# Cosformer attention and a mixture of adapters on one core: q scaled by a diagonal on TensorE, k scaled on GpSimd, attention numerators in row tiles

## The chip, the cores and the metric

The kernel runs on one core of one Trainium2 chip. The metric is the device time of one execution in microseconds (us). A core has a matrix engine (TensorE, PE in the profile; its weight loads are shown apart as PEld), VectorE (DVE), ScalarE (ACT), GpSimd (POOL), a queue engine (SyncE, SP) and 16 DMA engines. Each engine executes its own instructions in the order in which they were put in its queue, and semaphores make an engine wait for another. Matmul results land in PSUM (eight banks of 2 KB per partition), everything else is in SBUF.

## The reference

Inputs are q, k and v of shape 8 x 8 x 576 x 64 (batch, head, position, channel), and the weights of eight adapters of rank 16 on 512 channels. Linear attention with cosine weights comes first:

```python
theta = np.pi / 2.0 * pos / S
def phi(x, c, s):
    r = np.maximum(x, 0.0)
    return np.concatenate([r * c, r * s], axis=-1)
q_p = phi(q, cos_w, sin_w)
k_p = phi(k, cos_w, sin_w)
kv = np.einsum('bhsf,bhsd->bhfd', k_p, v)
z = np.sum(k_p, axis=2)
num = np.einsum('bhsf,bhfd->bhsd', q_p, kv)
den = np.einsum('bhsf,bhf->bhs', q_p, z)[..., None] + 1e-06
return (num / den).astype(np.float32)
```

Its output, as 4608 rows x of 512 channels, goes through the adapters: the two largest of eight gate logits `x @ w_gate` are chosen, a softmax over the two gives weights w, and the result is `x + sum over the two of w * ((x @ A[e]) @ B[e])`.

## The kernel before

**Layout.** A load puts one batch of q, k or v in SBUF as [128, G=4, NS=9, 64]: the partitions are two heads of a pair times 64 position blocks r, and position r * 9 + s lies at index s. So one s of one batch is a set of 64 positions of all eight heads. cos_tab and sin_tab hold, for each partition and s, the cosine and the sine of the position.

**A tile n** (NT = 36) is 128 output rows: two sets of 64. Nine tiles make a pair of batches 2m and 2m+1: four tiles of the first batch, four of the second, and a mixed one (s = 8 of both).

**k side, once per batch.** scale_k writes kp = max(k * cos, 0) and max(k * sin, 0), one instruction each per s (L141; batch 0 has the cosines on ScalarE, L139). kv (L155) multiplies kp with v and a column of ones, eight matmuls per s, each over the 64 partitions of one head, so that the two heads of a pair stand in different row halves of the array; it sums in kvz (two PSUM banks) over all nine s. kv_out copies the sums to SBUF (L162).

**q side, per tile.** scale_q (L168) makes four scaled pieces qp on VectorE; transp_q (L177) transposes them in eight matmuls with the identity into qpTp, a single bf16 PSUM bank; evac_q (L184) copies that to SBUF in one instruction of 1024 elements. numden (L197, L202) puts a small constant in the denominators and multiplies: per head one matmul over all 128 features (64 of cosine, 64 of sine). Its result nd takes two PSUM banks and has one buffer.

**Behind it.** normalise (L209, L211) divides, giving xt. transp_x (L219) and evac_x (L225) make its transpose, logits (L239) multiplies that with adapters and gate weights together. For a group of three tiles gate_a (L248 to L257), gate_sig (Sigmoid, L265) and gate_b (L272, L274) choose and weight the adapters, transp_z (L282) and evac_z (L288) transpose the result. delta (L294, L295) adds x and the adapters' second product in PSUM (dx, one bank), evac_o (L303) copies it out, store (L311) writes it by two DMAs on SP.

**Order.** The order within each engine's queue is written out by hand: the loop over n calls the helpers one after another, and each engine takes its instructions in that order. Iteration n holds normalise(n), the numerators of n+1, the transposes of x(n), scaling and transposing of q(n+2), and an older tile's delta. In the kernel before, logits of a whole group come in one iteration, gate_a at its end, gate_sig at the top of the next and gate_b at that one's end. Lists (scale_at, kv_at) place three s of scale_k and kv in six of nine iterations. All loads but k of batch 0 and the weights are issued by GpSimd, which converts fp32 to bf16 on the way, all ahead of the loop; the weights come by SP as fp32 and are cast on VectorE (L327 to L330).

## Time and profile before

| | us |
|---|---|
| median of 3 runs (148.26 to 149.88) | 149.34 |
| the profiled execution | 149.11 |
| its span, first to last instruction | 147.3 |

The profile is of one execution. Its page gives the busy time of each engine, then the chain of work that ended last, followed back from the last instruction, then the costliest groups of instructions: line, engine, operation, output and inputs, shapes, count, then busy us and mean ns of one, and the idle time of the engine ahead of them with what ended it. A timeline row gives the start in us, the duration of the row, the engine, the line and the operation; "x8" are eight instructions in a row, and what stands in brackets is the engine's idle time before, with its releaser. Durations overlap on an engine: where one instruction's end is not waited for, the next starts earlier, and the step from start to start is what the engine needs. TensorE's granted clock is 0.98 over the span, and the DMA engines are over 90% busy for the first 85 us or so:

| us from the start | PE | DVE | ACT | POOL |
|---|---|---|---|---|
| 50 to 60, busy | 8.09 | 9.36 | 6.22 | 1.48 |
| 100 to 110, busy | 8.14 | 8.72 | 6.72 | 0.00 |

### The profile page before, as it was taken

How to read it: one execution, taken by the hardware profiler on the slowest of the kernel's cores; microseconds unless marked ns; L12 is line 12 of the kernel's file. 1: busy time of each engine (PE TensorE's matmuls, PEld its weight loads, DVE VectorE, ACT ScalarE, POOL GpSimd, SP SyncE). 2: the span in 40 equal slices, each digit the busy share in tenths (PEclk: the TensorE clock that was granted, in tenths of full speed). 3: DMA queues.
4: the chain of work that ended last, by engine and by line, in shares of the span. 5: the costliest groups of instructions: out<-in, count | busy, mean ns of one | idle time of the engine just before them, and what ended most of it. 6: DMA issues, size and time to landing. Idle time of an engine off the chain costs nothing.

```text
span 147.3 us, 4206 instructions
## 1 busy us (share of the span) xinstructions
PE 103.9 (71%) x1652; PEld 73.6 (50%) x1652; DVE 110.7 (75%) x483; ACT 88.5 (60%) x143; POOL 18.1 (12%) x31
## 2 busy tenths in 40 slices
PE   0019589856878788778788788688877887777540
PEld 0018468744655555555466456346654556464110
DVE  3251799868798798798896987987988987866400
ACT  7370155767457757596476566875584577875540
POOL 6922322232222222000000000000000000000000
PEclk9999999999999999999999999999999999999975
DMA  4999999999999999999999933143333332534783
GB/s 100 320 204 233 208 209 207 208 208 207 207 239 237 236 238 240 237 237 242 261 229 231 232 77 83 46 104 71 75 72 76 71 87 65 122 93 111 166 205 92
DMA packets 19780, 25.00 MB, mean 170 GB/s; under 512 B 2736, under 2 KB 14512, under 8 KB 19760
## 3 DMA queue, kind: packets, MB, share of 16 engines
q0 software_dynamic: 12144, 13.57, 53.7%
q1 hardware_dynamic: 7616, 11.16, 29.1%
q8 instruction: 13, 0.21, 0.6%
q14 instruction: 7, 0.06, 0.1%
HBM read 28.85 MB, written 9.44 MB: 260 GB/s over the span
## 4 chain that ended last, share of the span: by engine, by line
DVE 43%; PE 29%; ACT 13%; DMA 6%; issue 5%; ACTq 0%; POOLq 0%
DVE kp L141 15%; DVE xt L211 11%; PE xz L219 7%; DMA v<-in_v_dram 6%; PE za L239 5%; PE qpTp L177 5%; ACT qpT L184 5%; PE nd L202 5%; PE kvz L155 4%; DVE qp L168 4%; ACT osb L303 4%; DVE zg L274 3%; ACT xT L225 3%; DVE m L248 2%; DVE rden L209 2%
## 5 line engine op out<-in xcount | busy, mean ns | idle before, releaser
L184 ACT COPY qpT<-qpTp 128x1024 bf16<-128x1024 bf16 x35 | 35.4, 1012 | 22.4 <-PE qpTp L177 22.4
L155 PE MATMUL kvz<-v,kp 64*128 64x128 bf16 x576 | 28.0, 236 | 13.6 <-DMA v<-in_v_dram 10.6
L225 ACT COPY xT<-xz 128x512 bf16<-128x512 bf16 x36 | 21.1, 585 | 18.4 <-PE xz L219 18.2
L155 PEld LDWEIGHTS <-kp 64*128 64x128 bf16 x576 | 18.9, 104 | 24.7 <-DVE kp L141 13.0
L219 PE MATMUL xz<-ident,xt 128*128 128x128 bf16 x144 | 15.3, 230 | 17.2 <-DVE xt L211 15.3
L211 DVE TENSOR_TENSOR xt<-nd,rden 128x512 bf16<-128x512 f32 x36 | 24.9, 692 | 1.3
L177 PE MATMUL qpTp<-ident,qp 128*128 128x128 bf16 x288 | 24.1, 230 | 1.2 <-DVE qp L168 1.2
L303 ACT COPY osb<-dx 128x512 f32<-128x512 f32 x36 | 21.3, 592 | 5.1 <-PE dx L295 4.3
L219 PEld LDWEIGHTS <-xt 128*128 128x128 bf16 x144 | 9.5, 118 | 25.2 <-DVE xt L211 24.9
L168 DVE TENSOR_SCALAR qp<-q,sin_tab 128x256 bf16<-128x256 bf16 x72 | 20.5, 285 | 0.0
L168 DVE TENSOR_SCALAR qp<-q,cos_tab 128x256 bf16<-128x256 bf16 x72 | 20.3, 282 | 0.0
L177 PEld LDWEIGHTS <-qp 128*128 128x128 bf16 x288 | 18.3, 102 | 2.0 <-DVE qp L168 1.5
L141 DVE TENSOR_SCALAR kp<-k,sin_tab 128x256 bf16<-128x256 bf16 x63 | 18.3, 291 | 0.0
L202 PE MATMUL nd<-kvsb,qpT 128*128 128x65 bf16 (+1 forms) x320 | 16.9, 197 | 1.4 <-DVE qpT L186 0.8
L141 DVE TENSOR_SCALAR kp<-k,cos_tab 128x256 bf16<-128x256 bf16 x63 | 17.9, 284 | 0.0
L294 PE MATMUL dx<-xt,ident 128*128 128x512 bf16 x36 | 13.8, 383 | 3.0 <-ACT osb L303 3.0
L295 PE MATMUL dx<-Ball,zgT 128*128 128x512 bf16 x36 | 14.0, 389 | 1.2 <-DVE zgT L288 0.4
L202 PEld LDWEIGHTS <-qpT 128*128 128x128 bf16 (+1 forms) x320 | 12.8, 101 | 2.1 <-DVE qpT L186 0.9
L197 PE MATMUL nd<-eps_hi,ones 128*128 128x4 bf16 x72 | 11.8, 172 | 0.0
L239 PE MATMUL za<-AW,xT 128*128 128x136 bf16 x144 | 10.6, 222 | 0.0
L248 DVE MAX8 m<-za 128x8 f32<-128x8 f32 x36 | 3.9, 162 | 8.6 <-PE za L239 8.5
L288 DVE COPY zgT<-xz 128x384 bf16<-128x384 bf16 (+2 forms) x13 | 4.4, 342 | 7.2 <-ACT xT L225 4.6
(44 smaller groups left out, 93.7 us busy)
## 6 DMA issues: line engine op xcount, KB each, us to landing
out_dram<-osb SPq DMA_DIRECT2D x72, 128.0 KB, 2.4
v<-in_v_dram POOLq DMA_DIRECT2D x8, 576.0 KB, 23.9
q<-in_q_dram POOLq DMA_DIRECT2D x8, 576.0 KB, 24.9
k<-in_k_dram POOLq DMA_DIRECT2D x7, 576.0 KB, 24.4
k0f<-in_k_dram SPq DMA_DIRECT2D x1, 1152.0 KB, 5.6
Af<-in_moe_A_dram SPq DMA_DIRECT2D x1, 256.0 KB, 11.2
Bf<-in_moe_B_dram SPq DMA_DIRECT2D x1, 256.0 KB, 12.3
Wf<-in_moe_w_gate_dram SPq DMA_DIRECT2D x1, 16.0 KB, 11.5
```

The source lines that it names most:

```text
L141: nc.vector.tensor_scalar(out=dst, in0=src, scalar1=tab[:, s:s + 1], scalar2=0.0, op0=ALU.mult, op1=ALU.max)
L155: nc.tensor.matmul(out=kvz_t[b][:, par, g], lhsT=kp_t[b][pr, s, g], rhs=v_rhs(b, g, s, pr), start=(s == 0 and g == 0), stop=(s == NS - 1 a ...
L168: nc.vector.tensor_scalar(out=qp[:, j, :, i, :], in0=q_b[b][:, :, s, :], scalar1=tab[:, s:s + 1], scalar2=0.0, op0=ALU.mult, op1=ALU.max)
L177: nc.tensor.transpose(out=t[:, j, 2 * g:2 * g + 2, :], in_=qp[:, j, g], identity=ident)
L184: nc.scalar.copy(t, src)
L202: nc.tensor.matmul(out=nd[pr, gg, j * W:(j + 1) * W], lhsT=qpT[:, h, js], rhs=kv_t[b][:, h % 2, h // 2, :], start=False, stop=(j == 3), sk ...
L211: nc.vector.tensor_tensor(out=xt, in0=nd[:, :, :, 0:D], in1=rden.rearrange("p (g j) -> p g j", g=2).to_broadcast([128, 2, 4, D]), op=ALU.mult)
L219: nc.tensor.transpose(out=xz[:, c * 128:(c + 1) * 128], in_=x[:, c], identity=ident)
L225: nc.scalar.copy(t, src)
L239: nc.tensor.matmul(out=za[:, i, :], lhsT=xT[:, c, :], rhs=AW[:, c, :], start=(c == 0 and i == 0), stop=(c == DCH - 1), skip_group_check=True)
L295: nc.tensor.matmul(out=dx, lhsT=zgT_t[g][:, n - groups[g][0], :], rhs=Ball, start=False, stop=True)
L303: nc.scalar.copy(t, src)
```

## The change

- **q.** scale_q is gone. transp_q(n, gp) makes half a tile: for each of two s, two ordinary matmuls with unscaled q as the stationary operand (64 columns, one head pair) and a moving operand of 256 columns, the diagonal matrices of cosine and sine. The two matmuls write the lower and the upper 64 PSUM partitions. The result is fp32, so that half a tile fills the one qpTp bank; evac_q applies the Relu while it copies 512 elements. There are two such halves per tile.
- **numden.** Features now lie so that one head's cosine part and its sine part are in different instructions: 16 matmuls over 64 partitions each, alternating between lower and upper row halves, which write different banks. kv_out rearranges kv for it, in two ScalarE and two VectorE copies.
- **k.** scale_k runs on GpSimd, a whole batch at a time, between the DMA issues; kp has three buffers. Batch 0 stays on ScalarE and VectorE. Loads of later batches are issued behind the scaling of earlier ones.
- **Weights** are loaded and cast by GpSimd's DMAs, behind v of batch 1. The combined weight block is [E + 1, DCH, 16] per partition, so logits has 144 columns for 136, in runs of 16.
- **Order.** Logits come per tile, in the iteration after their tile. gate_a, gate_sig and gate_b follow each other in one iteration, ahead of logits. The numerators of n+1 come ahead of the transposes of x(n); evac_x is on VectorE; delta stands between the two q halves; kv of batch 2m+1 comes one iteration later. The diagonals are built on VectorE ahead of batch 0's scaling, and forty matmuls on a block of ones come first on TensorE.

```diff
@@ transposing and scaling q @@
+    diag = persist.tile([128, NS, 2, 128], BF16, name="diag")
+    def make_diag(s):
+        for i, tab in enumerate((cos_tab, sin_tab)):
+            nc.vector.tensor_scalar(out=diag[:, s, i], in0=ident, scalar1=tab[:, s:s + 1],
+                                    scalar2=None, op0=ALU.mult)
...
-    def transp_q(n):
-        qpT_t[n] = t = ps.tile([128, 2, H, HALF], BF16, name="qpTp", tag="qpTp")
-        qp = qp_t.pop(n)
-        for j in range(2):
-            for g in range(G):
-                nc.tensor.transpose(out=t[:, j, 2 * g:2 * g + 2, :], in_=qp[:, j, g],
-                                    identity=ident)
+    def transp_q(n, gp):
+        qpT_t[n, gp] = t = ps.tile([128, 2, 2, 128], FP32, name="qpTp", tag="qpTp")
         for j, (b, s) in enumerate(tokens(n)):
+            for gl, pr in enumerate((lo, hi)):
+                nc.tensor.matmul(out=t[pr, j], lhsT=q_b[b][:, 2 * gl + gp, s, :],
+                                 rhs=diag[:, s], start=(j == 0), stop=True,
+                                 skip_group_check=True)
...
+        qpT_t[n, gp] = t = p_qpt.tile([128, 4, 2, HALF], BF16, name="qpT")
         if eng == "act":
-            nc.scalar.copy(t, src)
+            nc.scalar.activation(t, src, AF.Relu)
@@ numden @@
+        for gp in range(2):
+            for par in range(2):
+                j = 2 * gp + par
+                for i in range(2):
+                    for gl, pr in enumerate((lo, hi)):
+                        for cols, js, b in jobs:
+                            nc.tensor.matmul(out=nd[cols, gl, j * W:(j + 1) * W],
+                                             lhsT=qpT[gp][pr, 2 * i + par, js],
+                                             rhs=kv_t[b][pr, i, gp, par], start=False,
+                                             stop=(j == 3 and i == 1), skip_group_check=True)
@@ kv_out @@
+        for i in range(2):
+            for gl, pr in enumerate((lo, hi)):
+                src = z[i * HALF:(i + 1) * HALF, :, gl, :, 0:W]
+                dst = t[pr, i].rearrange("p gp t w -> p t gp w")
+                if gl == i:
+                    nc.scalar.copy(dst, src)
+                else:
+                    nc.vector.tensor_copy(dst, src)
@@ the weights @@
+    def load_weights():
+        nc.gpsimd.dma_start(out=AW[:, 0:E].rearrange("p e c r -> p e (c r)"),
+                            in_=A.rearrange("e (p c) r -> p e (c r)", c=DCH))
+        nc.gpsimd.dma_start(out=AW[:, E, :, 0:E],
+                            in_=w_gate.rearrange("(p c) e -> p c e", c=DCH))
+        nc.gpsimd.dma_start(out=Ball, in_=Bw.rearrange("e r d -> (e r) d"))
@@ the schedule, as it stands after the change @@
+        for s in range(6):
+            make_diag(s)
+        wu = ps.tile([128, DM], FP32, name="dx")
+        for i in range(40):
+            nc.tensor.matmul(out=wu[:, 0:128], lhsT=ones, rhs=ones, start=True, stop=True)
         for s in range(NS):
+            scale_k(0, s, ("act" if s < 7 else "dve", "dve"))
             kv(0, s)
+        for s in range(6, NS):
+            make_diag(s)
+        load_v(1)
+        load_weights()
+        load_q(1)
+        for s in range(NS):
+            scale_k(1, s)
+        for b in (2, 3):
+            load_k(b)
+            load_v(b)
+            load_q(b)
         kv_out(0)
+        for n in range(2):
+            for gp in range(2):
+                transp_q(n, gp)
+                evac_q(n, gp, "act" if gp == 0 else "dve")
         numden(0)
...
         for n in range(NT + 8):
             live = n < NT
+            if n % 9 in (1, 5):
+                b = 2 * (n // 9) + (2 if n % 9 == 1 else 3)
+                if b < B:
+                    for s in range(NS):
+                        scale_k(b, s)
+                    if b + 2 < B:
+                        load_k(b + 2)
+                        load_v(b + 2)
+                        load_q(b + 2)
+            ready = [g for g, t in enumerate(groups) if t[-1] + 2 == n]
             moved = [g for g, t in enumerate(groups) if t[-1] + 3 == n]
             if live:
                 normalise(n)
+            for b, s in kv_at.get(n, ()):
+                kv(b, s)
+                if s == NS - 1:
+                    kv_out(b)
             if n + 1 < NT:
                 numden(n + 1)
             if live:
+                transp_x(n)
             if n + 2 < NT:
+                transp_q(n + 2, 0)
+                evac_q(n + 2, 0)
             for g in moved:
                 evac_z(g)
                 todo += groups[g]
+            if live:
+                evac_x(n, "dve")
             for d in todo[:1] if live else todo:
                 delta(d)
                 evac_o(d)
                 store(d)
             del todo[:1 if live else None]
+            if n + 2 < NT:
+                transp_q(n + 2, 1)
+                evac_q(n + 2, 1)
             for g in ready:
                 gate_a(g)
+                gate_sig(g)
+            for g in ready:
                 gate_b(g)
+            if 0 < n <= NT:
+                logits(n - 1)
+            for g in ready:
                 transp_z(g)
```

More of the change, by code (lines that the diff above doesn't have):

```diff
@@ L27 @@
     W = D + 1
-    ZW = ER + E
+    ZW = ER + R
     DCH = DM // 128
@@ L172, in transp_q @@
[L172 to L182 removed]
+        kv_t[b] = t = p_kv.tile([128, 2, 2, 2, W], BF16, name="kvsb")
@@ L231, with logits @@
     group_of = {n: g for g, t in enumerate(groups) for n in t}
-    def logits(g):
-        za_t[g] = za = ps.tile([128, 3, ZW], FP32, name="za",
-                               tag="qpTp" if g == len(groups) - 1 else "za")
-        for i, n in enumerate(groups[g]):
-            xT = xT_t.pop(n)
-            for c in range(DCH):
-                nc.tensor.matmul(out=za[:, i, :], lhsT=xT[:, c, :], rhs=AW[:, c, :],
-                                 start=(c == 0 and i == 0), stop=(c == DCH - 1),
-                                 skip_group_check=True)
+    def logits(n):
+        g = group_of[n]
+        i = n - groups[g][0]
+        if i == 0:
+            za_t[g] = ps.tile([128, 3, ZW], FP32, name="za",
+                              tag="qpTp" if g == len(groups) - 1 else "za")
+        xT = xT_t.pop(n)
+        for c in range(DCH):
+            nc.tensor.matmul(out=za_t[g][:, i, :], lhsT=xT[:, c, :], rhs=AW[:, :, c, :],
+                             start=(c == 0 and i == 0), stop=(c == DCH - 1),
+                             skip_group_check=True)
     def gate_a(g):
         n = len(groups[g])
-        l = za_t[g][:, 0:n, ER:ZW]
+        l = za_t[g][:, 0:n, ER:ER + E]
         m8 = p_g.tile([128, 3, 8], FP32, name="m8")
```

97 lines of the change are left out of this document (21 added, 76 removed).

## The prediction

> **What bounds the kernel now.** I read the page first (busy times, chain of waits), then the timeline of two stretches of the loop, then the groups of instructions by line for the price of each operation.
>
> ```profile
> span 147.3 us, 4206 instructions
> ...
> PE 103.9 (71%) x1652; PEld 73.6 (50%) x1652; DVE 110.7 (75%) x483; ACT 88.5 (60%) x143; POOL 18.1 (12%) x31
> ...
> DVE 43%; PE 29%; ACT 13%; DMA 6%; issue 5%; ACTq 0%; POOLq 0%
> DVE kp L141 15%; DVE xt L211 11%; PE xz L219 7%; DMA v<-in_v_dram 6%; PE za L239 5%; PE qpTp L177 5%; ACT qpT L184 5%; PE nd L202 5%; PE kvz L155 4%; DVE qp L168 4%; ACT osb L303 4%; DVE zg L274 3%; ACT xT L225 3%; DVE m L248 2%; DVE rden L209 2%
> ```
>
> VectorE is the busiest engine and 43% of the chain, and the k scaling (kp, L141) is its largest piece. But no engine is full, so the order of the queues matters. One loop iteration without k scaling looks so in the timeline:
>
> ```profile
> 63.15 0.41 PE L219 MATMUL xz<-ident,xt 128*128 128x128 bf16 x4 [0.88 <-DVE xt L211]
> ...
> 63.40 0.17 PE L197 MATMUL nd<-eps_hi,ones 128*128 128x4 bf16 x1
> ...
> 63.70 0.64 PE L177 MATMUL qpTp<-ident,qp 128*128 128x128 bf16 x8
> ...
> 64.17 0.38 PE L294 MATMUL dx<-xt,ident 128*128 128x512 bf16 x1
> ...
> 64.42 1.01 ACT L184 COPY qpT<-qpTp 128x1024 bf16<-128x1024 bf16 x1 [0.24 <-PE qpTp L177]
> ...
> 65.33 0.60 ACT L303 COPY osb<-dx 128x512 f32<-128x512 f32 x1
> 65.46 0.41 PE L219 MATMUL xz<-ident,xt 128*128 128x128 bf16 x4 [0.50 <-DVE xt L211]
> ```
>
> This is a ring through TensorE and ScalarE: x transposed 0.25 (63.15 to 63.40), numerator matmuls 0.30, q transposed 0.47, 0.25 until ScalarE starts, 1.01 of evacuation, 0.03 back to TensorE: 2.31 us, the whole step to 65.46. It closes because each queue is in order: the next numerator needs the evacuated q. Where k is scaled, VectorE is slower than the ring:
>
> ```profile
> 66.80 0.28 DVE L141 TENSOR_SCALAR kp<-k,cos_tab 128x256 bf16<-128x256 bf16 x1
> ...
> 66.99 0.28 DVE L141 TENSOR_SCALAR kp<-k,sin_tab 128x256 bf16<-128x256 bf16 x1
> ```
> ```profile
> 59.98 0.41 PE L219 MATMUL xz<-ident,xt 128*128 128x128 bf16 x4 [0.45 <-DVE xt L211]
> ...
> 90.45 0.41 PE L219 MATMUL xz<-ident,xt 128*128 128x128 bf16 x4 [0.44 <-DVE xt L211]
> ```
>
> Nine iterations take 30.47 us, 3.39 each; 36 scalings start 0.195 apart and make 7.0 of it. Taking those away alone would leave 23.4. What the change puts in their place decides.
>
> **The change part by part.** Times of PE are steps from one start to the next; the rows for its rates and for the gate:
>
> ```profile
> 60.52 0.87 PE L239 MATMUL za<-AW,xT 128*128 128x136 bf16 x12
> ...
> 61.23 0.61 PE L177 MATMUL qpTp<-ident,qp 128*128 128x128 bf16 x8
> ```
> ```profile
> 44.59 0.33 PE L282 MATMUL xz<-ident,zg 128*128 128x128 bf16 x3
> 44.85 0.45 PEld L155 LDWEIGHTS <-kp 64*128 64x128 bf16 x16
> ```
> ```profile
> 132.18 0.17 PE L197 MATMUL nd<-eps_hi,ones 128*128 128x4 bf16 x1
> ...
> 132.28 0.32 PE L202 MATMUL nd<-kvsb,qpT 128*64 128x65 bf16 x8
> ...
> 132.52 0.18 PE L197 MATMUL nd<-eps_hi,ones 128*128 128x4 bf16 x1
> ```
> ```profile
> L303 ACT COPY osb<-dx 128x512 f32<-128x512 f32 x36 | 21.3, 592 | 5.1 <-PE dx L295 4.3
> ...
> L202 PE MATMUL nd<-kvsb,qpT 128*64 128x65 bf16 x64 | 2.5, 201 | 0.0
> ```
>
> *q scaling.* VectorE loses 4 x 0.195 = 0.78 us per tile. TensorE gets 8 matmuls of 256 columns for 8 transposes of 128 (0.47/8 = 0.059 each, so 0.11 at 256). A half-tile is four, in two column tiles. In the row at 132.28 eight column-tiled matmuls start (0.32 - 0.20)/7 = 0.017 apart, faster than their 65 columns at the transposes' rate (0.030): pairs overlap. So a half-tile costs 0.22 if pairs overlap, 0.44 if not; I take 0.22.
>
> *Two evacuations instead of one.* The result is fp32, fills the one qpTp bank with half a tile, and is evacuated by two Relus of 512 elements, each like L303: 0.59. Both halves use one buffer, and the second transposition stands on TensorE behind the wait for the first evacuation. Start of the first half at 0: 0.22 issue, 0.25 to ScalarE, 0.59, 0.06 back, 0.22 second half: 1.34; then 0.25 and 0.59: 2.18 is the end of the second evacuation, call it E. The output evacuation between them takes ScalarE's free time; delta hides in TensorE's wait.
>
> *Numerators in row tiles.* 16 matmuls of 64 rows for 8 of 128. kv, row-tiled already, loads 16 weights in 0.45 (0.025 each with the tail taken off); 0.017 is the column-tiled row. I take 0.02, so 0.32 per tile.
>
> *Tile forms alternate.* Between full matmul and column tiles the rows show 0.10 into them (0.03 is usual) and 0.52 - 0.40 = 0.12 out (last of the eight starts at 132.40): 0.08 more per switch. L282 to kv (44.70 to 44.85) is of that size. After the change the loop has the order kv, eps, numerators, x transposes, q half, delta, q half, logits: up to six switches on the path. The Trainium skill, TensorEngine Tiling (Array Packing), Key Properties, says that changing the tiling mode drains TensorE; an array emptied fully would cost more than these rows show, and that is a rival below.
>
> *Cycles.* Plain: E + 0.06, second half of the numerators 0.16, switch, x transposes 0.25, switch: 2.81. With 24 kv matmuls TensorE itself is late: 1.34, logits 4 x 0.059 = 0.25 (slightly wider now), kv 0.60, eps 0.06, numerators 0.32, x 0.25, six switches 0.48: 3.30. Before, kv ran in the time VectorE took for kp; now nothing covers it.
>
> *The gate.* Before, Sigmoid came first in ScalarE's next iteration. Now it stands behind the second evacuation, and on VectorE gate_b waits for it with the next normalisation queued behind, which frees the one nd buffer:
>
> ```profile
> 131.61 0.59 ACT L303 COPY osb<-dx 128x512 f32<-128x512 f32 x1
> 132.09 0.23 ACT L265 ACTIVATE u<-tg 128x24 f32<-128x24 f32 x1
> ```
> ```profile
> 132.35 0.18 DVE L272 TENSOR_TENSOR em<-u,mask 128x24 f32<-128x24 f32 x1 [0.49 <-ACT u L265]
> 132.57 0.56 DVE L274 TENSOR_TENSOR zg<-za,em 128x384 bf16<-128x384 f32 x1
> 133.04 0.20 DVE L209 RECIPROCAL rden<-nd 128x8 f32<-128x8 f32 x1
> 133.28 0.69 DVE L211 TENSOR_TENSOR xt<-nd,rden 128x512 bf16<-128x512 f32 x1
> ```
>
> Sigmoid starts 0.11 before E (0.48 after the copy ahead of it); from its start to the end of xt is 133.97 - 132.09 = 1.88; TensorE goes on at E + 1.83 = 4.01 with eps, numerators, x and three switches 0.87: 4.88. With kv behind it: logits wait for zg (E + 0.99 = 3.17), then logits 0.25, z transposes 0.17, kv 0.60, eps to x 0.63, five switches 0.40: 5.22. Once in three iterations.
>
> *kv_out* becomes two ScalarE and two VectorE copies of 64 x 260. Bounds for each: 0.23 (Sigmoid, 24 elements) and L162 below; I take 0.4. In one iteration of nine the next numerators need it at once: +0.85. The mixed tile has 16 matmuls more: +0.32.
>
> Nine iterations: 4 x 3.30 + 2 x 5.22 + 4.88 + 2 x 2.81 + 0.85 + 0.32 = 35.3, or 3.92 each against 3.39.
>
> ```profile
> 20.67 1.04 PE L177 MATMUL qpTp<-ident,qp 128*128 128x128 bf16 x8
> ...
> 130.00 0.61 PE L177 MATMUL qpTp<-ident,qp 128*128 128x128 bf16 x8
> ```
> ```profile
> 142.71 0.58 ACT L303 COPY osb<-dx 128x512 f32<-128x512 f32 x1 [1.08 <-PE dx L295]
> ```
>
> These rows bound 33 iterations: 109.3 now. After: 3 x 35.3, the last six (without batch 8) 3.30 + 5.22 + 4.15 + 2.81 + 4.88 + 2.81 = 23.2, less the gate that iteration 1 lacks (1.9): 127.2, so +17.9.
>
> *The end.* From 130.00 to the last evacuation are 12.7 us. Two of the last gates now queue Sigmoid behind output evacuations (each delta and evacuation about 1.3); I add 3, between 0 and 5.
>
> *k scaling on POOL, and its queue.*
>
> ```profile
> masks.py:199 POOL TENSOR_SCALAR_AFFINE_SELECT ident<-ident 128x128 bf16<-128x128 bf16 x1 | 0.3, 304 | 0.0
> ...
> masks.py:197 POOL MEMSET ident<- 128x128 bf16 x1 | 0.2, 204 | 0.1
> ```
> ```profile
> L59 POOL DMA_DIRECT2D q<-in_q_dram x8 | 6.0, 750 | 12.2 <-DMA k<-in_k_dram 12.2
> ...
> L162 ACT CAST kvsb<-kvz 128x520 bf16<-128x520 f32 x8 | 4.7, 593 | 5.5 <-PE kvz L155 5.5
> ```
>
> No elementwise scaling on POOL is in the trace. Twice the 128-element rows bounds it from 0.41 to 0.61; two operations in one could double the upper. I take 0.6: 18 x 0.6 plus three issues of 0.75 is 13 us per batch, under the 17.6 of 4.5 iterations, so it is hidden, and so are the loads behind it. It would bind from 0.85 us. The Trainium skill, GPSIMD Engine Reference, Performance versus the Vector engine, has 2.6 cycles per element measured for a two-input op; at its 1.2 GHz 256 elements would be an estimated 0.55 us, no bound either; no run here shows it yet.
>
> *The start.*
>
> ```profile
> 10.56 4.02 PE L155 MATMUL kvz<-v,kp 64*128 64x128 bf16 x72 [10.56 <-DMA v<-in_v_dram]
> ```
>
> kv waits for v; three weight loads on SP no longer share its time. The 72 matmuls cost 0.056 each against 0.025 later, and the forty warm-up matmuls may mend some of that. But twelve diagonals precede k on VectorE, and four halves must alternate before the first numerators. I take -1.5, between 0 and -4. The weights, moved from SP to POOL behind k1 and v1, are needed only in iteration 1.
>
> *Sum.* Profiled time 149.11 (span 147.3 and 1.8 around it; the median shown is 149.34): 149.1 + 17.9 + 3 - 1.5 = 168.5.
>
> **Rivals.** *Column tiles don't overlap:* 2 x 0.22 per iteration, 33 times, +14.5: 183. Against it the 0.017; but there two different operands met.
>
> *Full drains:* if the array empties at every switch, one costs a matmul's whole 0.20 less 0.03. About 41 switches in nine iterations lie on the path; 0.09 more each makes 3.7, in 33 iterations 13.5: 182. The rows at 132.4 speak for half of it. (That is the Trainium skill's rule on mode switching, taken literally.) With free switches it would be 12 less, 156.5; with a cheaper start and end, 151.
>
> *POOL binds:* at 1.0 us a scaling, 20.3 us per batch; seven batches from about 16 us (v at 10.56 less 1.3, then q and k at some 3.5 each, an estimate) end at 158, four iterations and the end follow: about 194. Above 0.85 it decides.
>
> *Faster:* VectorE's relief counts, because Sigmoid's wait vanishes: if gate_b were served before E, all nine iterations would be plain or kv ones: 6 x 3.30 + 3 x 2.81 + 1.17 = 29.4, some 106 in 33 iterations; with free switches too 26.1, some 94: 149.1 - 15 - 1.5 = 133. It decides where the wait costs under about 0.2 us with the switches as priced, 1.2 with free ones. For it speaks the 43% of VectorE; against it ScalarE's order, written out.
>
> *Not what it says:* Relu and Sigmoid reload ScalarE's tables in turn.
>
> ```profile
> L265 ACT ACT_TABLE_LOAD x1 | 1.3, 1283 | 0.0
> ```
>
> 24 loads of 1.28 would give 199. Against it: the Relus of batch 0 needed no load.
>
> **Numbers.** Forecast 0.51; column tiles 0.12; full drains 0.07; POOL 0.10; tables 0.02; near even 0.05; faster 0.13. The range of 149 to 187 leaves out the faster case, half of POOL's and the tables. Its inner part, 156 to 177, is the forecast's own. Faster by over 1% (about what a measurement tells from none) 0.13, within 1% 0.04, slower 0.83.
>
> **What would show it.** L155's wait for kp gone; ScalarE waiting twice per tile for the q matmuls; VectorE's idle before em (L272's successor) about 1 us, with the Sigmoid right behind the second Relu; iterations of about 2.8, 3.3 and 5; POOL scalings of 0.4 to 0.6 with no one waiting. Wrong if plain iterations are under 2.5, if normalisation doesn't wait at gates, or if kv waits for POOL.

## The result and the profile after

| | before | after |
|---|---|---|
| median, us | 149.47 (148.26 to 149.88, 4 runs) | 213.35 (212.74 to 215.37, 4 runs) |
| ratio, 95% interval | 1 | 1.432 [1.419, 1.444] |
| profiled execution, us | 149.11 | 212.74 |
| its span, us | 147.3 | 211.0 |
| TensorE's mean granted clock in it | 0.98 | 0.85 |

Ratios leave out executions over 1.5% slower than the fastest of their kernel. The other three executions of after had a granted clock of 0.765 to 0.778 and took 213.08 to 215.37.

The change makes the kernel slower, as forecast, but by 64 us and not by 19; 213 lies far outside the range. From the page of after, the busy times, and from the slices POOL and TensorE's clock (tenths, 5.3 us each):

```profile
span 211.0 us, 4873 instructions
...
PE 138.6 (66%) x1989; PEld 87.8 (42%) x2012; DVE 83.0 (39%) x284; ACT 75.3 (36%) x148; POOL 161.1 (76%) x160
...
POOL 7509999799999999999999999999999950000000
PEclk9999998555997699999965999999857999969555
```

The clock's slices of before (3.7 us each):

```profile
PEclk9999999999999999999999999999999999999975
```

VectorE did lose its work (110.7 to 83.0 us) and is now idle most of the time. Two things are new. GpSimd works almost without a pause from the fourth slice to the thirty-third, and then has nothing left. And TensorE's clock, which before stayed at 9 tenths or more until the last two slices, falls to half again and again. The groups by line, of after:

```profile
L145 POOL TENSOR_SCALAR kp<-k,cos_tab 128x256 bf16<-128x256 bf16 x63 | 71.5, 1134 | 9.4 <-DMA k<-in_k_dram 9.3
...
L159 PE MATMUL kvz<-v,kp 64*128 64x128 bf16 x576 | 26.5, 245 | 18.3 <-POOL kp L145 15.2
...
L173 DVE CAST kvsb<-kvz 64x260 bf16<-64x260 f32 x16 | 6.8, 426 | 27.5 <-ACT kvsb L171 27.3
...
L171 ACT CAST kvsb<-kvz 64x260 bf16<-64x260 f32 x16 | 6.0, 374 | 27.8 <-PE kvz L159 20.3
```

One scaling on GpSimd takes 1.13 us, where VectorE started one every 0.195. TensorE's kv waits 15.2 us for it in all. The kv_out copies have the durations forecast (0.37 and 0.43 for 0.4), but VectorE's follow on ScalarE's, which ended 27.3 us of VectorE's idle time, though neither reads what the other writes. GpSimd's timeline, its first scaling and its last:

```profile
16.23 1.14 POOL L145 TENSOR_SCALAR kp<-k,cos_tab 128x256 bf16<-128x256 bf16 x1 [8.01 <-DMA k<-in_k_dram]
...
170.61 1.13 POOL L145 TENSOR_SCALAR kp<-k,sin_tab 128x256 bf16<-128x256 bf16 x1
```

126 scalings and the DMA issues between them fill the 155.5 us from 16.23 to 171.74: 22.4 per batch where three loads are issued too. The sum had 13 per batch, and room for 17.6 in 4.5 iterations. Four iterations and the end follow, so a kernel with this pace cannot end much before 210. Those iterations, with nothing to wait for on GpSimd, show the ring as it is (timeline; 171.64 to 176.78 has a kv_out, 176.78 to 179.67 is plain, 179.67 to 184.56 has a gate):

```profile
171.64 0.41 PE L179 MATMUL qpTp<-diag,q 128*64 128x256 bf16 x4
...
174.38 0.37 ACT L171 CAST kvsb<-kvz 64x260 bf16<-64x260 f32 x1 [0.48 <-PE kvz L159]
...
174.79 0.88 DVE L173 CAST kvsb<-kvz 64x260 bf16<-64x260 f32 x2 [1.51 <-ACT kvsb L171]
...
175.71 0.38 ACT L171 CAST kvsb<-kvz 64x260 bf16<-64x260 f32 x1 [0.95 <-DVE kvsb L173]
...
176.13 0.37 PE L209 MATMUL nd<-kvsb,qpT 64*128 64x65 bf16 x13 [0.22 <-ACT kvsb L171]
...
176.78 0.41 PE L179 MATMUL qpTp<-diag,q 128*64 128x256 bf16 x4
...
177.29 0.60 ACT L187 ACTIVATE qpT<-qpTp 128x512 bf16<-128x512 f32 x1 [1.21 <-PE qpTp L179]
...
177.94 0.41 PE L179 MATMUL qpTp<-diag,q 128*64 128x256 bf16 x4 [0.21 <-ACT qpT L187]
...
178.44 0.60 ACT L187 ACTIVATE qpT<-qpTp 128x512 bf16<-128x512 f32 x1
...
179.67 0.41 PE L179 MATMUL qpTp<-diag,q 128*64 128x256 bf16 x4
...
181.83 0.21 ACT L275 ACTIVATE u<-tg 128x24 f32<-128x24 f32 x1
182.07 0.18 DVE L282 TENSOR_TENSOR em<-u,mask 128x24 f32<-128x24 f32 x1 [1.14 <-ACT u L275]
...
183.74 0.19 PE L201 MATMUL nd<-eps_hi,ones 128*128 128x4 bf16 x2 [0.26 <-DVE xt L219]
...
184.56 0.41 PE L179 MATMUL qpTp<-diag,q 128*64 128x256 bf16 x4
```

The plain iteration takes 2.89 (summed: 2.81) and the gate's 4.89 (summed: 4.88). The one with kv_out takes 5.14 (summed: 4.15): the four copies run on ScalarE, VectorE twice and ScalarE, one after the other, 1.75 us from 174.38 until TensorE goes on at 176.13.

### The profile page after: what moved, and what is told of

It reads as the page before. It is cut to its first block, busy times and chain, and to the rows that moved or that the text cites. A ratio compares the mean times of both kernels' runs of the same rounds, so it can differ in the third digit from the quotient of the medians.

```text
span 211.0 us, 4873 instructions
## 1 busy us (share of the span) xinstructions
PE 138.6 (66%) x1989; PEld 87.8 (42%) x2012; DVE 83.0 (39%) x284; ACT 75.3 (36%) x148; POOL 161.1 (76%) x160
## 5 line engine op out<-in xcount | busy, mean ns | idle before, releaser
L145 POOL TENSOR_SCALAR kp<-k,cos_tab 128x256 bf16<-128x256 bf16 x63 | 71.5, 1134 | 9.4 <-DMA k<-in_k_dram 9.3
L187 ACT ACTIVATE qpT<-qpTp 128x512 bf16<-128x512 f32 x70 | 41.8, 597 | 86.7 <-PE qpTp L179 84.3
L145 POOL TENSOR_SCALAR kp<-k,sin_tab 128x256 bf16<-128x256 bf16 x63 | 71.3, 1133 | 0.0
L179 PE MATMUL qpTp<-diag,q 128*64 128x256 bf16 x288 | 35.1, 327 | 11.6 <-ACT qpT L187 10.9
L159 PE MATMUL kvz<-v,kp 64*128 64x128 bf16 x576 | 26.5, 245 | 18.3 <-POOL kp L145 15.2
L235 DVE COPY xT<-xz 128x512 bf16<-128x512 bf16 x36 | 15.2, 422 | 48.8 <-PE xz L227 48.7
L249 PE MATMUL za<-AW,xT 128*128 128x144 bf16 x144 | 17.1, 249 | 20.5 <-DVE zg L284 20.5
L179 PEld LDWEIGHTS <-q 128*64 128x64 bf16 x288 | 14.8, 119 | 31.5 <-issue 29.3
L209 PE MATMUL nd<-kvsb,qpT 64*128 64x65 bf16 (+1 forms) x640 | 21.4, 213 | 5.4 <-ACT kvsb L171 2.1
L249 PEld LDWEIGHTS <-xT 128*128 128x128 bf16 x144 | 10.8, 106 | 29.5 <-issue 27.1
L209 PEld LDWEIGHTS <-qpT 64*128 64x128 bf16 (+1 forms) x640 | 14.9, 111 | 8.1 <-issue 5.4
L173 DVE CAST kvsb<-kvz 64x260 bf16<-64x260 f32 x16 | 6.8, 426 | 27.5 <-ACT kvsb L171 27.3
```

The costliest lines, as they stand in the source:

```text
L145: e.tensor_scalar(out=dst, in0=src, scalar1=tab[:, s:s + 1], scalar2=0.0, op0=ALU.mult, op1=ALU.max)
L159: nc.tensor.matmul(out=kvz_t[b][:, par, g], lhsT=kp_t[b][pr, s, g], rhs=v_rhs(b, g, s, pr), start=(s == 0 and g == 0), stop=(s == NS - 1 a ...
L179: nc.tensor.matmul(out=t[pr, j], lhsT=q_b[b][:, 2 * gl + gp, s, :], rhs=diag[:, s], start=(j == 0), stop=True, skip_group_check=True)
L187: nc.scalar.activation(t, src, AF.Relu)
L209: nc.tensor.matmul(out=nd[cols, gl, j * W:(j + 1) * W], lhsT=qpT[gp][pr, 2 * i + par, js], rhs=kv_t[b][pr, i, gp, par], start=False, stop= ...
L235: nc.vector.tensor_copy(t, src)
```

## The experiments

Each time is one execution, with the kernel before at 148.3 to 149.0 beside it, unless a number of executions is named; then it is their median. POOL PACE and Q PATH were the first two theories: either GpSimd's slow scaling sets the time, or the loop around q does.

**1. No k scaling.** On after.

```diff
-        for s in range(NS):
-            scale_k(1, s)
+        for b in range(1, B):
+            kp_t[b] = kp_t[0]
...
-                    for s in range(NS):
-                        scale_k(b, s)
```

> The changed kernel without any scaling of k for batches 1 to 7: their kv matmuls read batch 0's scaled k, so the output is not the reference's; the loads of later batches stand where they stood. Theory POOL PACE (GpSimd's 1.12 us per scaling holds the loop, all else goes as the prediction's cycles): 170 to 180 us, the cycles of about 2.9, 3.2 and 5 that the changed kernel shows between its waits, all the way through. Rival Q PATH (the alternation of TensorE and ScalarE is much dearer than summed, and GpSimd only late beside it): 195 or more. Rival FASTER LOOP (without GpSimd VectorE's relief counts): under 145.

199.73. GpSimd's pace is worth 13.6 us of 64; the other 50 stay without it. The clock was 0.77, as in the other three executions of after.

**2. k on VectorE.** All loads ahead of the loop, k scaled as before, three s an iteration.

```diff
-            if n % 9 in (1, 5):
...
+            for b, s in kv_at.get(n + 1, ()):
+                scale_k(b, s, ("dve", "dve"))
             for g in ready:
                 gate_b(g)
```

> The changed kernel with k of batches 1 to 7 scaled on VectorE, three positions per iteration ahead of gate_b, and all loads issued ahead of the loop. POOL PACE: VectorE idles over 1.5 us per iteration in the ring of TensorE and ScalarE, so 6 scalings of 0.195 cost little: 172 to 184 us. Rival VECTORE AGAIN (k scaling on VectorE is on the path as before, 7 us per nine iterations): 28 us above the run without scaling, about 200.

197.73, no more than with no scaling at all: in this order VectorE has the room for it. Moving it to GpSimd bought nothing.

**3. Half of k on GpSimd.** Cosines there, in batches and with the late loads as in after; sines on VectorE as in 2.

```diff
+                        scale_k(b, s, part=(0,))
...
+                scale_k(b, s, ("dve", "dve"), part=(1,))
```

> The changed kernel with the cosine half of k's scaling left on GpSimd and the sine half on VectorE. POOL PACE: 9 x 1.12 and three issues of 0.78 are 12.4 us per batch, less than the 18 us of 4.5 iterations, so GpSimd no longer holds anything: within 5 us of the run with k on VectorE. Rival LATE LOADS (not the pace but the issue of the loads behind the scalings holds the loop): still 195 or more, kv waiting for v or q. Rival PORT (VectorE's scalings lengthen GpSimd's): GpSimd's 1.13 us mean rises over 1.4.

197.51, as 2. So neither the late loads nor GpSimd's working beside VectorE costs time that single executions could show, though VectorE's scalings lengthened from 0.291 to 0.346 us; the full pace does.

**4. The kernel before, with k on GpSimd.**

```diff
             for b, s in scale_at.get(n, ()):
-                scale_k(b, s)
+                scale_k(b, s, ("pool", "pool"))
```

> The kernel before with one part of the change alone: k of batches 1 to 7 scaled on GpSimd, with loads, order and q path as before. POOL PACE: GpSimd is done with its issues at about 24 us, then 126 scalings of 1.12 end at 165, and six iterations and the end of some 30 us follow: 190 to 202. Rival Q PATH (GpSimd's pace matters only beside the new q path): under 150, faster than before since VectorE loses 28 us. Rival PORT (VectorE's scalings of q, which are left, lengthen GpSimd's): over 1.3 us each and 210 or more.

224.59, where 190 to 202 was expected. The time is in PORT's range, but the scalings took 1.14 and 1.15 us and not over 1.3. The chain by engine and line, and GpSimd's timeline:

```profile
POOL 63%; DMA 20%; PE 6%; issue 4%; ACT 3%; DVE 2%; POOLq 1%; ACTq 0%
POOL kp L142 60%; DMA k<-in_k_dram 10%; DMA v<-in_v_dram 10%; ACT osb L304 2%; POOL q L59 1%; PE za L240 1%; PE xz L220 1%; PE dx L295 1%; PE qpTp L178 1%; PE nd L203 1%; POOL v L59 1%; PE dx L296 1%; POOL k L59 1%; PE kvz L156 1%; DVE xt L212 1%
```
```profile
51.59 0.74 POOL L59 DMA_DIRECT2D q<-in_q_dram  x1 [2.11 <-DMA k<-in_k_dram]
52.37 1.16 POOL L142 TENSOR_SCALAR kp<-k,cos_tab 128x256 bf16<-128x256 bf16 x1
```

The first scaling stands in GpSimd's queue behind the last load, and that load is issued only at 51.59, when an earlier one has landed; the expectation had 24. The loads, which cost nothing in the kernel before, are in the way once GpSimd computes. The change had moved them behind the scalings, and was right in that.

**5. The gate apart.** On 2: logits of a group one iteration after its last tile, gate_a and Sigmoid in the next, gate_b in the one after that.

```diff
-            for g in ready:
-                gate_b(g)
-            if 0 < n <= NT:
-                logits(n - 1)
+            for g in full:
+                for d in groups[g]:
+                    logits(d)
...
+            for g in gated:
+                gate_b(g)
```

> r2 (k on VectorE, 197.7 us) with the gate in pieces: logits of a whole group one iteration after its last tile, gate_a and the Sigmoid at the end of the next, gate_b behind evac_x of the one after, so that no engine waits for another inside an iteration. Theory GATE AND CLOCK (each gate stall costs 2 us, and the idle TensorE then loses its clock, which makes the cycles after it longer): 11 x 2 = 22 us and some 10 of the slow clock less: 160 to 172, granted clock above 0.9. GATE ALONE: 174 to 178, clock as in r2 (0.79). RING (the stalls are not what holds it): above 188.

180.11, 17.6 less than 2, with the clock at 0.86 for 0.79: outside the ranges of all three theories. Sigmoid's place costs time, as the prediction counted; how much of the 17.6 is the stalls themselves and how much the clock this run doesn't separate.

**6. kv_out paired.** On 2, the copies in an order in which ScalarE and VectorE can run side by side.

```diff
-        for i in range(2):
-            for gl, pr in enumerate((lo, hi)):
+        for i, gl in ((0, 0), (1, 0), (1, 1), (0, 1)):
```

> r2 with the four copies of kv_out in another order, so that ScalarE and VectorE read different partition halves at the same time. In the changed kernel they ran one after another, 1.7 us between the first copy's start and the last one's end. Theory SERIAL COPIES: 0.8 us less in each kv_out that the next numerators wait for, four of eight, and a little in the others: 3 to 6 us under r2, 192 to 195. Rival: the copies are hidden or serial for another reason: 196 to 199.

197.01, no gain that one execution can show. From the waits (total, times, longest):

```profile
DVE kvsb L172 <- ACT kvsb L170: 10.8, 16, 3.1
```

Each of the 16 VectorE copies still waits for one of ScalarE's. They read the same two PSUM banks of kvz and write one shared tile. The timeline of before shows that a shared destination isn't needed for it:

```profile
65.91 0.58 ACT L225 COPY xT<-xz 128x512 bf16<-128x512 bf16 x1
...
66.53 0.36 DVE L288 COPY zgT<-xz 128x384 bf16<-128x384 bf16 x1 [0.34 <-ACT xT L225]
```

These two copies read different columns of the one bank xz and write different tiles, and VectorE still waits until ScalarE has ended (in all, 11 of its 13 such copies wait so). So a common source in PSUM is enough; whether the bank itself or the order that the program sets between the two copies holds them apart stays open.

**7. Filler.** On 2, products of the ones block that nobody uses: 24 at each gate, 16 behind each kv_out, where TensorE only waits.

```diff
+                    fill(16)
...
+            if ready and live:
+                fill(24)
```

> r2 with useless matmuls added on TensorE, 24 of 128 columns in each gate stall and 16 behind each kv_out; everything else is as it was. Theory CLOCK (TensorE idles in the stalls, its granted clock halves for 3.4 us or more, and the following work is slower): the granted clock rises above 0.9 and the time falls by 8 to 20 us, to 178 to 190. Rival EFFECT ONLY (the low clock follows from waiting and costs nothing on the path): 197 to 203, a little slower by the added work.

186.64: 376 more matmuls make it 11 us faster. The clock of 2, then of 7:

```profile
PEclk9955558555797599999966969999879786697855
```
```profile
PEclk9968556957999999999999999999999999999855
```

TensorE's timeline of 2 shows how little idling it took:

```profile
31.59 0.41 PE L179 MATMUL qpTp<-diag,q 128*64 128x256 bf16 x4 [0.75 <-ACT qpT L187]
31.93 0.42 PE L249 MATMUL za<-AW,xT 128*128 128x144 bf16 x4
32.29 0.84 PE L159 MATMUL kvz<-v,kp 64*128 64x128 bf16 x24
...
33.60 0.19 PE L209 MATMUL nd<-kvsb,qpT 64*128 64x65 bf16 x1 [0.33 <-ACT kvsb L171]
...
35.40 0.61 PE L227 MATMUL xz<-ident,xt 128*128 128x128 bf16 x4
...
37.90 0.66 PE L249 MATMUL za<-AW,xT 128*128 128x144 bf16 x4
```

At 31.93 four logits matmuls take 0.42, at 37.90 four take 0.66; the four x transposes at 35.40 take 0.61 (0.41 at the full clock). The granted clock was 1.00 from 31 to 34 us and 0.51 from 34 to 37. It fell behind a stretch with TensorE busy for 1.87 of 3.00 us, whose longest idle time is 0.75. The Trainium skill, TensorE: Matmul & The Clock Gate, Why this matters for your kernels, asks that no idle gap between bursts of matmuls be over some 3 us. These rows show that shorter gaps, often enough, lower the clock too.

**8. GpSimd's prices.** On 1, three of each of ten operations on GpSimd behind the loads.

```diff
+        for r in range(3):
+            two(o16[:, :, 0, :], src[:, :, 0, :])
+            two(oflat[:, 0:256], flat[:, 0:256])
...
+            nc.gpsimd.tensor_copy(oflat[:, 0:256], flat[:, 0:256])
```

> The kernel of r1 (no k scaling beyond batch 0, output not the reference's), all loads ahead, and then on GpSimd, that has nothing else to do, three rounds of ten test instructions on spare tiles: the kernel's scaling (multiply and maximum, 256 elements in runs of 64), the same contiguous, with 128, 512 and 1024 elements, in fp32, with the multiplication alone, with the maximum alone, and plain copies in bf16 and fp32. Theory PER ELEMENT: the price is some 4 ns an element: 0.6, 1.1, 2.1 and 4.1 us, the same for runs and contiguous. Rival START (a fixed price per instruction): 0.9 or more at 128. PER OPERATION: one operation alone takes 0.6 or less. CONVERSION: fp32 takes 0.6 or less.

The groups by line and shape (count, then busy us and mean ns of one):

```profile
L367 POOL TENSOR_SCALAR poflat<-q,cos_tab 128x1024 bf16<-128x1024 bf16 x3 | 11.1, 3700 | 0.3
...
L367 POOL TENSOR_SCALAR po<-pf,cos_tab 128x256 f32<-128x256 f32 x3 | 3.4, 1140 | 0.0
L367 POOL TENSOR_SCALAR poflat<-q,cos_tab 128x256 bf16<-128x256 bf16 x3 | 3.4, 1136 | 0.0
L376 POOL TENSOR_SCALAR po<-q,cos_tab 128x256 bf16<-128x256 bf16 x3 | 2.8, 929 | 0.0
...
L367 POOL TENSOR_SCALAR poflat<-q,cos_tab 128x128 bf16<-128x128 bf16 x3 | 2.1, 712 | 0.3
...
L380 POOL COPY poflat<-q 128x256 bf16<-128x256 bf16 x3 | 1.2, 396 | 0.2
```

L367 multiplies and takes the maximum, L376 only multiplies. From 128 to 1024 elements it is (3700 - 712) / 896 = 3.33 ns an element and 0.28 us of start. Type and layout make no difference, one operation in place of two saves 0.2, and a copy costs a third. (This run, with no k scaled in the loop, took 201.49.)

**9. No scaling, filler.** 1 and 7 together: no k scaling, and a warm clock.

```diff
+                    fill(16)
...
+            if ready and live:
+                fill(24)
```

> r1 (no scaling of k beyond batch 0, output not the reference's) with r7's useless matmuls on TensorE in the gate stalls and behind kv_out. It is the loop of the prediction's sum with nothing from GpSimd and a warm TensorE. Theory SUM HOLDS AT FULL CLOCK: 168.5, and 0.9 more for each of eight kv_outs since the copies run one after another: 170 to 178, clock above 0.9. Rival SUM SHORT ANYWAY (switches, waits or the gate are dearer than summed): 183 or more at that clock.

186.61, clock 0.95. Without GpSimd and without a cold clock it is still 18 over the forecast: the sum itself is short. And 7, which scales all of k on VectorE, is no slower (186.64).

**10. No kv_out.** On 9.

```diff
-                    kv_out(b)
-                    fill(16)
+                    kvz_t.pop(b)
+                    kv_t[b] = kv_t[0]
```

> r9 (no k scaling, filler in the gate stalls) without the copies kv_out of batches 1 to 7 and without the filler behind them: all tiles read batch 0's kv, so the output is not the reference's. Theory KV_OUT (nine iterations of r9 take 2.5 us more than summed, and both kv_outs in them stand 1.7 us on the path where the sum has 0.85 once): 3.3 us less per nine iterations, seven copies of 1.7 or 12 us in all: 173 to 177. Rival (the excess over the sum lies elsewhere, in switches or waits): 181 or more.

174.02: seven kv_outs cost 12.6, or 1.8 each, the stretch that the timeline of after shows between 174.38 and 176.13. (The filler that went with them cost nothing: with it the iteration took 5.13 in 9, without it 5.14 in after.)

**11. After, with the filler.** 7's two lines on after itself.

```diff
+                    fill(16)
...
+            if ready and live:
+                fill(24)
```

> The changed kernel with r7's useless matmuls in the gate stalls and behind kv_out, so that TensorE stays warm and GpSimd alone is left as it was. Theory POOL LAST: GpSimd ends its 126 scalings at 171.7 whatever TensorE does, and iterations 30 to 35 and the end follow: 207 to 213, all of the clock's 11 us hidden by GpSimd. Rival INDEPENDENT COSTS (clock and GpSimd add up): 198 to 204.

210.41, only 3 less. GpSimd's last scaling:

```profile
171.01 1.13 POOL L145 TENSOR_SCALAR kp<-k,sin_tab 128x256 bf16<-128x256 bf16 x1
```

It is where it was (170.61 in after). A warm clock saves time only until kv waits for GpSimd again.

**12 and 13. A better order for q on TensorE.** On 5, q transposed three tiles ahead, kv between the two q halves and some filler (4 executions); then, on that, evac_x on ScalarE (4 executions).

```diff
-            if n + 2 < NT:
-                transp_q(n + 2, 0)
-                evac_q(n + 2, 0)
+            if n + 3 < NT:
+                transp_q(n + 3, 0)
+                evac_q(n + 3, 0)
...
+            for b, s in kv_at.get(n + 1, ()):
+                kv(b, s)
```
```diff
-                evac_x(n, "dve")
+                evac_x(n, "act")
```

> r5 (k on VectorE, gate in pieces, 180.1 us) with q transposed three tiles ahead in place of two, kv between the two q halves, filler matmuls in the first six iterations, and q of batch 1 loaded ahead of the weights. Theory RING (the numerators wait for the evacuation that has just been started; TensorE alone needs some 2.9 us per iteration): 138 to 150 us, clock above 0.95. Rival PE BOUND (switches and matmuls fill TensorE whatever the order): 160 or more.

> r10 with x evacuated on ScalarE as before the change, since VectorE has k again. Theory: VectorE sets the pace of the iterations with k scaling, so 0.35 less there shortens 20 of 36 iterations: 3 to 7 us under r10. Rival: TensorE sets it: within 1 us of r10; or ScalarE comes late with the q halves: above r10.

186.72 (184.16 to 190.12), 1.243 [1.231, 1.256] of before, and 173.42 (172.5 to 175.16), 1.164 [1.155, 1.173]. The first was meant to reach 138 to 150 and came out slower than 5. By the ratios the second gained 12 where 3 to 7 was expected. Why the first failed was not settled; the waits of both name the chain from the numerators through VectorE's normalisation back to TensorE (total, times, longest), first of the one, then of the other:

```profile
PE nd L201 <- DVE xt L219: 31.0, 27, 2.8
```
```profile
PE nd L201 <- DVE xt L219: 18.7, 19, 2.8
```

With evac_x off VectorE that wait is 12 us shorter. But the profiled executions, 190.12 and 172.50, are 17.6 apart, and the first is the slowest of its four, so not all of the 12 need be evac_x. No order tried with q on TensorE came under before.

**14. The kernel before, two of three cosines of k on ScalarE** (4 executions).

```diff
-                scale_k(b, s)
+                scale_k(b, s, ("dve" if s % 3 == 0 else "act", "dve"))
```

> The kernel before with two of three cosine scalings of k on ScalarE, in its idle time behind the output evacuation, for batches 1 to 7. Theory VECTORE BINDS BEFORE: each scaling taken away saves 0.195 on VectorE, 42 of them 8 us: 139 to 144. Rival SCALARE (0.41 each, 0.8 per iteration, delays the evacuations of the ring): 148 or more.

166.62 (163.4 to 169.16) against 148.94. From the groups and the waits of this run (167.16):

```profile
L139 ACT ACTIVATE kp<-k,cos_tab 128x256 bf16<-128x256 bf16 x42 | 19.2, 512 | 0.0
```
```profile
PE kvz L155 <- ACT kp L139: 20.2, 21, 1.2
```

The 42 scalings put 19.2 us on ScalarE, which stands in the ring, and TensorE's kv waits 20.2 us for them. The loss is 17.7 by the medians; the fastest execution, at a clock of 0.98 like that of before, still lost 14.5, so the clock is at most the smaller part of it. Relief of VectorE doesn't pay for this.

**15 and 16. The kernel before, with a warm start,** 130 products of ones first (10 executions); then also the weights loaded behind q of batch 1 and cast in iteration 3 (10 executions).

```diff
+        for i in range(130):
+            nc.tensor.matmul(out=wu[:, 0:128], lhsT=ones, rhs=ones, start=True, stop=True)
         for s in range(NS):
```
```diff
-    nc.sync.dma_start(out=Bf, in_=Bw.rearrange("e r d -> (e r) d"))
...
+            nc.gpsimd.dma_start(out=Bf, in_=Bw.rearrange("e r d -> (e r) d"))
...
+            if n == 3:
...
+                nc.vector.tensor_copy(Ball, Bf)
```

> The kernel before with one small part of the change enlarged: 130 matmuls on a block of ones ahead of all else on TensorE, until v lands. Theory CLOCK AT THE START: the 72 kv matmuls go at 0.027 in place of 0.056 and the next few steps are shorter: 2 to 4 us faster, 145 to 147. Rival: the warm-up delays the first matmuls or the clock falls again: 148 to 151.

> r14 with the three weight loads moved from SP to GpSimd's queue behind q of batch 1, as in the change but without the cast, and their casts on VectorE into iteration 3. v of batch 0 then lands about 1.4 us earlier, as it did after the change (9.11 for 10.56): 1 to 2 us under r14. Rival: q of batch 0 sets the start: within 0.7 of r14.

149.03, ratio 1.000 [0.996, 1.005], and 147.54, ratio 0.997 [0.993, 1.001]: no difference from before that the intervals show, though the second is 1.5 under the first, as expected. Its kv starts only 0.25 earlier (10.29, right behind the warm-up, for 10.54); its first q scaling, no longer behind the casts, starts at 12.79 for 15.16. In the timeline of the first:

```profile
10.54 2.19 PE L155 MATMUL kvz<-v,kp 64*128 64x128 bf16 x72
...
14.82 0.43 DVE L333 CAST Ball<-Bf 128x512 bf16<-128x512 f32 x1 [1.23 <-DMA Bf<-in_moe_B_dram]
15.16 0.28 DVE L168 TENSOR_SCALAR qp<-q,cos_tab 128x256 bf16<-128x256 bf16 x1
```

Warm, kv of batch 0 takes 2.19 for 4.02, but the first scaling of q stood behind a cast that waits for its load, so the 1.8 us went into another wait: the q scaling starts at 15.16, in before at 15.26.

**17 and 18. The second of these, with one of three or two of three cosines of k on GpSimd** from batch 2 on (4 executions each).

```diff
-                scale_k(b, s)
+                scale_k(b, s, ("pool" if b >= 2 and s % 3 == 2 else "dve", "dve"))
```
```diff
-                scale_k(b, s, ("pool" if b >= 2 and s % 3 == 2 else "dve", "dve"))
+                scale_k(b, s, ("pool" if b >= 2 and s % 3 != 0 else "dve", "dve"))
```

> r15 (kernel before, warm start, weights later) with one of three cosine scalings of k on GpSimd, batches 2 to 7: 18 scalings of 1.13, 20 us in all, far under GpSimd's capacity. Theory: VectorE binds the kernel before and each scaling taken off it saves 0.195: 3.5 us less than r15, 143 to 145.5. Rival PORT (GpSimd at work lengthens VectorE's own scalings, as in r4 where they rose from 0.28 to 0.37): 146.5 to 150.

> The same with two of three cosine scalings, 36 of 1.13, 41 us. Theory: 7 us less than r15, 139.5 to 143. Rival PORT: as r17 or above, 145 to 150. Rival LATE (GpSimd has two scalings of 1.13 per iteration and the last is needed in it): kv waits for kp, above 150.

163.99, ratio 1.106 [1.102, 1.109], and 164.41, ratio 1.111 [1.108, 1.114]. GpSimd's timeline and TensorE's waits, of the first:

```profile
52.37 0.74 POOL L59 DMA_DIRECT2D q<-in_q_dram  x1 [2.11 <-DMA k<-in_k_dram]
53.14 6.81 POOL L143 TENSOR_SCALAR kp<-k,cos_tab 128x256 bf16<-128x256 bf16 x6
```
```profile
PE kvz L157 <- POOL kp L143: 18.0, 1, 18.0
```

It is 4's queue again: one wait of 18 us, a little more than the 16.45 lost against the version without it. PORT is not the cause: VectorE's scalings took 0.288 to 0.303 us. That GpSimd could take a third of the cosines with its loads out of the way was not tried. No version found beats before.

## Why the prediction was right or wrong

The sum, as three parts, from rows of the timeline: the start up to the q transposition that stood at 20.67 before, 33 iterations, and from there to the start of the last output evacuation.

| us | summed | after | 1: no scaling | 9: and warm | 10: and no kv_out |
|---|---|---|---|---|---|
| start | 19.2 | 21.88 | 21.01 | 21.64 | 21.13 |
| 33 iterations | 127.2 | 166.14 | 153.96 | 141.45 | 129.39 |
| end | 15.7 | 18.12 | 18.12 | 16.92 | 16.90 |

In after these rows bound the parts:

```profile
21.88 0.64 PE L179 MATMUL qpTp<-diag,q 128*64 128x256 bf16 x4
...
188.02 0.64 PE L179 MATMUL qpTp<-diag,q 128*64 128x256 bf16 x4
...
206.14 0.59 ACT L313 COPY osb<-dx 128x512 f32<-128x512 f32 x1 [1.88 <-issue]
```

Together the sum is short of after by 2.7 + 38.9 + 2.4 = 44.0 us, the whole distance from 168.5 to the profiled 212.7. Taken away in the order of the columns, the iterations lose 12.2 with GpSimd's scaling, 12.5 with the cold clock and 12.1 with kv_out. The order matters, since the first two hide each other: with the clock warmed first (11), GpSimd is worth 210.4 - 186.6 = 23.8.

**What held.** The direction, and its reason: VectorE's 43% of the chain was not worth having, because the ring through TensorE and ScalarE grew with a second evacuation. Experiments 1 and 2 show it from the other side, and 9 and 7 with the filler: with k back on VectorE the time is no longer than with no scaling of k at all. Plain and gate iterations measured 2.89 and 4.89 for 2.81 and 4.88. Column tiles overlap, or the plain iteration would have shown 0.44 more. Full drains at 0.09 more each would have made it 2.99 (two changes of form on its path), and an iteration with kv 3.84 (six); in 9, at a clock of 0.95, that one took 3.46 (100.66 to 104.12), for 3.30 summed. Relu and Sigmoid did not reload tables by turns (one load at the Sigmoid in the whole run). v came earlier, as said. One reading was off, without effect on the sum: in before the x transposes at 65.46 wait for VectorE's xt, as the row's bracket says, and don't wait for ScalarE. They stand outside the ring, which without their 0.25 is 2.06.

**The step that failed first: "I take 0.6"** for a scaling on GpSimd. It measured 1.13, almost four times the upper of the two rows (0.30, for half the elements). The prediction had said that two operations could double the upper bound of 0.61, to 1.2, and that GpSimd would bind from 0.85; but it took the lower value, gave the rival a chance of 0.10, and priced it at 194. The 1.2 came near by luck: a second operation adds only 0.2, and a multiplication alone takes 0.93 (8). Its own sign of being wrong, kv waiting for POOL, came with 15.2 us. Those rows were a memset and a mask; neither multiplies, nor chains two operations. A row that is near in shape need not be near in work. By the Trainium skill's page, GPSIMD Engine Reference, Performance versus the Vector engine, the estimate was 0.55; the runs show 1.13, and 3.33 ns an element. The Trainium skill's section 4.1 of that page, Engine selection, calls one-input operations there "roughly line-rate", next to VectorE; here the step from one scaling's start to the next is 1.115 against VectorE's 0.195.

**The term that was mis-sized: kv_out,** "+0.85" in one iteration of nine. The durations were right, but the four copies were taken to run in two pairs. They run singly, 1.75 us, and two kv_outs in nine iterations stand ahead of numerators on the path, not one. In the 33 iterations the sum had 4 x 0.85 = 3.4; experiment 10 takes 12.1 out of them: 8.7 too little. What is left between 127.2 - 3.4 = 123.8 and 129.4 is 5.6, or 0.17 an iteration. That is of the size of the small errors of the cycles (plain 0.08; with kv 0.16), and was not taken apart further.

**The thing left out: the clock.** Every step of the sum took durations from a kernel with a granted clock of 0.98. The iterations that it forecast had stalls in them, of 1.83 us at each gate, and the sum took it for granted that TensorE would come out of them at the speed at which it went in. Experiment 7 shows the cost with everything else in place: 11.1 us of 197.7. In after most of it hides behind GpSimd: the filler there gains 2.9 (11), and three executions of after at a clock of 0.765 to 0.778 took at most 2.6 longer than the one at 0.85.

**Start and end.** "-1.5, between 0 and -4" became +1.2 (20.67 to 21.88). kv of batch 0 did start 1.45 earlier, at 9.11, but kv_out now runs ahead of the first q evacuation on ScalarE, and the forty warm-up products did not warm the clock: the 72 matmuls took 4.02 again. "+3" for the end became 5.4.

The range failed because of what its rivals were. Its upper end, 187, left room for column tiles (183) or full drains (182), and neither came. GpSimd, which came, was priced at 194 for 1.0 us a scaling and half left out of the range; at the measured 1.13 it ends later still. Four serial copies in every kv_out and a lower clock stood among no rivals, and the three that came make most of the 44 us together: without them (10) the kernel is 5.5 us over the forecast.

## What to carry to other kernels

Before work is moved to an engine, price it by a row of the same kind of operation on that engine, and where there is none, let the engine's break-even time (here 0.85 us) and not the middle of the bounds set the forecast. When a change lengthens TensorE's waits in a loop, price its work at the clock that a loop with such waits is granted and not at the clock of the kernel before. Look at whether copies that are meant to run side by side wait for each other. Work on GpSimd stands in the same queue as the DMA issues, so the loads must be ordered around it.

## What was not expected of the hardware

- A stretch of TensorE work with no idle time over 0.75 us, busy for 1.87 of 3.00 us, was enough for the clock to fall to half (2), and 376 products that nobody uses raised the mean from 0.79 to 0.91 (7).
- ScalarE's and VectorE's copies out of the same two PSUM banks, into different partitions, ran one after the other in both orders tried. In before, copies out of one bank into different tiles did so too. The cause is left open.
- Outstanding loads kept GpSimd's queue from its scalings until 52 us in experiment 4 and 53 us in 17, with 2.1 us of waiting ahead of the last issue.
- With GpSimd at work on k (4), VectorE's scalings of q took 0.377 us (sine) and 0.363 us (cosine), against 0.285 and 0.282 in the kernel before.
